# Both products of a block join over four 32x32 tiles instead of two, a state update with 48 stationary columns, and an order of work planned anew

## The chip, the cores and the metric

The kernel runs on one core of a Trainium2 chip. The metric is the device time of one execution in microseconds (us), here the median of three runs. The engines named below are TensorE (PE; its weight loads, which overlap the matmuls, are listed as PEld), VectorE (DVE), ScalarE (ACT), GpSimd (POOL) and SyncE (SP). SP computes nothing and issues most of the DMA transfers.

## The reference

Four batches, eight heads, 768 tokens, head size 48, all in float32. A DeltaNet layer keeps one 48x48 state per batch and head and goes through the tokens in order:

```
k_n = k / (norm(k) + 1e-6)
for t in range(S):
    y[t]  = q[t] @ state
    v_old = state.T @ k_n[t]
    state = state + beta[t] * outer(k_n[t], v[t] - v_old)
```

The heads of `y` are then laid side by side (4 x 768 x 384), and a MetaFormer block with an identity mixer follows: normalise each token over its 384 numbers, multiply by `g_ln`, `relu(xn @ w_ch1) @ w_ch2` with a hidden width of 1536, and add `y` back.

## The kernel before

**Chunks.** The tokens are cut into 12 chunks of 64. Inside a chunk the recurrence becomes matrix products for each of the 32 batch-and-head pairs ("heads" from here on): with the state S at the chunk's start, `ks = K S` and `qs = Q S` (line 1160), `u = X (v - ks)` (line 1215), `y = qs + P u` (line 1222), and `S += K^T u` (line 1232, the function `state_up`). P is the masked product of queries and keys (`queries`, line 963), and X is the inverse of a unit triangular 64x64 matrix built from the chunk's keys and beta (`gram`, line 963). Heads lie in two halves of 64 partitions, 16 heads (`GH`) to a half. On tiles of 64x64 of the TensorE array, two halves by two, each of these products is 32 matmuls in the source; the trace has two records for every float32 matmul, so a product appears as 64, and below it is said to have 64.

**The inverse.** For chunks 2 to 11 two chunks are inverted together in `rows_inverse`. The 64x64 triangle is cut into two 32x32 diagonal blocks and one block beside them. The diagonal blocks of two chunks are laid one to a partition by DMA (64 heads times two blocks), and VectorE inverts them row by row with a multiply (line 1045, into `tmp`) and a subtract (line 1050, into `xb`), 31 pairs for a block of 32. The planner counts each pair as one step. The result goes back to the layout of the products through DRAM (`xd<-xb`, then eight transfers `xt<-xd`).

**The join.** `join(c)` then fills the remaining 32x32 block: a transpose on VectorE (line 1103), a product E (line 1110), an eviction with a change of sign on ScalarE into `es` (line 1120), a product Z (line 1115) and an eviction into `xt` (line 1125). Each product is again 64 recorded matmuls: 16 heads by two halves, the halves named by `e`, and two records for each. `quad(n)` is the n-th group of 32 partitions. All inputs of E lie in quads 0 and 2. All its outputs go to quads 1 and 3 of one PSUM bank:

```
for h in range(GH):
    for e in range(2):
        nc.tensor.matmul(p[quad(2 * e + 1), h], gs[quad(2 * e), h, BK:C], xnj[quad(2 * e), h])
```

So E uses two of the array's 32x32 tiles, and Z, from quads 1 and 3 to quads 0 and 2, two others. Each product is evicted in two instructions of 32 partitions by 512 elements. Chunks 1 to 11 go through `join`. Chunk 1 also has `blocks_join`, which works one level lower, on 16x16 inverses; its two products of 128 recorded matmuls (lines 1077 and 1082) already run over four 32x32 tiles, from quad a to quad a. Chunk 1's own product `u` goes partly (line 1184) from quads 1 and 3, each to both of quads 1 and 3, with 48 moving columns.

**The MLP.** Chunks 0 to 2 use a plain first layer (line 1483). From chunk 3 on the first layer runs in `eleven` (line 1416) and from chunk 1 on the second in `seven` (line 1584), schemes that replace matmuls by sums on VectorE, ScalarE and GpSimd. They consist of full 128x128 matmuls on TensorE.

**The order of the work.** Every instruction is given to a planner (`Line`) as a step with an engine, an assumed cost, the buffers that it reads and writes, and optionally a due time. `schedule` goes backward from the due times (`DUE`, one for each chunk's MLP, and a slope) to a priority `pr` for each step; `run` then simulates the engines, the DMA queues, a port that it takes VectorE and GpSimd to share, and the fetching of TensorE's instructions (`BLOCK`, `FETCH`, `STALL`), and at each moment picks the ready step with the earliest `pr`. The order found is the order of the instructions in each engine's queue. On the chip each engine then works strictly in that order. Line 1662 is a dummy product on zeros that the planner puts where TensorE would sit idle early in the kernel. Line 555 is the helper that issues all DMAs.

## Time and profile before

| | |
|---|---|
| time, median of three runs | 560.05 us (558.03 to 564.31) |
| span of the profiled execution | 559.0 us |
| TensorE busy | 525.5 us, 94% of the span |
| VectorE, GpSimd, ScalarE busy | 370.3, 253.2 and 192.1 us |
| mean granted TensorE clock | 0.980 |
| DMA traffic | 54.65 MB, 98 GB/s |

The page of the profile gives busy time for each engine, the span in 40 slices of 14 us each, the chain of work that ended last, and groups of instructions by line. A row of such a group names the line, the engine, what is written and from what, the shape, the count, the busy time, the mean duration in nanoseconds of one instruction and the idle time before it. Small matmuls are pipelined: one takes 0.19 us from start to end, but the next starts a few nanoseconds later, so what a product of 64 of them costs is read from its first start and last end, not from the mean duration of one.

### The profile page before, as it was taken

The numbers are of one execution on the slowest core, as the hardware profiler recorded it, in microseconds if no ns is written. First come the engines' busy times: TensorE is split into PE (matmuls) and PEld (weight loads), VectorE is DVE, ScalarE is ACT, GpSimd is POOL, SyncE is SP. The second block draws the span as 40 slices with busy tenths as digits, with TensorE's granted clock in tenths as the row PEclk, the third lists the DMA queues.
The fourth block names the chain that finished last, engine by engine and source line by source line (L and its number), as shares of the span: only waits on it lengthen the run. The fifth ranks groups of instructions, "written<-read, shape, count | busy, mean of one in ns | idle before, by whom it ended". The sixth has DMA issues, their size and how long they took to land.

```text
span 559.0 us, 23060 instructions
## 1 busy us (share of the span) xinstructions
PE 525.5 (94%) x10060; PEld 478.8 (86%) x10060; DVE 370.3 (66%) x884; ACT 192.1 (34%) x452; POOL 253.2 (45%) x399
## 2 busy tenths in 40 slices
PE   7668869899998999899999999999999999999996
PEld 4547657678987899899999999999999999999996
DVE  5666549991689936889858968668777436253331
ACT  5667644232232324232323332513322224323030
POOL 5252337407885656267270352452352522426242
PEclk9898899999998999899999999999999999999999
DMA  9784784269454786553652543834404410111101
GB/s 177 265 158 128 195 219 64 44 149 168 55 86 71 139 195 86 106 100 83 162 77 50 99 81 77 191 46 81 94 15 103 106 30 33 32 48 40 28 1 28
DMA packets 195972, 54.65 MB, mean 98 GB/s; under 512 B 186136, under 2 KB 189344, under 8 KB 195872
## 3 DMA queue, kind: packets, MB, share of 16 engines
q1 hardware_dynamic: 190112, 40.39, 37.8%
q10 hardware_dynamic: 3552, 9.63, 5.0%
q0 software_dynamic: 2208, 3.17, 3.2%
q8 instruction: 78, 1.28, 1.0%
q14 instruction: 22, 0.18, 0.1%
HBM read 36.38 MB, written 16.78 MB: 95 GB/s over the span
## 4 chain that ended last, share of the span: by engine, by line
PE 78%; DVE 7%; DMA 6%; SPq 4%; issue 2%; ACT 1%; POOL 0%; DVEq 0%; POOLq 0%; ACTq 0%
PE f L1584 28%; PE f L1416 25%; PE f L1483 6%; SPq L555 4%; PE two L963 4%; DVE xb L1050 2%; DVE tmp L1045 2%; PE by L1222 2%; PE two L1215 2%; PE by L1160 2%; PE two L1160 2%; DMA gd<-gsb 2%; PE two L1232 2%; PE f L1505 1%; PE by L1115 1%
## 5 line engine op out<-in xcount | busy, mean ns | idle before, releaser
L1584 PE MATMUL f<-w_sb,h_all 128*128 128x192 f32 x396 | 95.0, 332 | 0.0
L1584 PE MATMUL f<-words,h_all 128*128 128x192 f32 x396 | 93.1, 328 | 0.0
L1570 POOL TENSOR_TENSOR h_all<-h_all 128x256 f32<-128x256 f32 x99 | 73.0, 742 | 43.3 <-PE f L1584 37.1
L1416 PE MATMUL f<-xnt,w_sb 128*128 128x128 f32 x648 | 88.8, 279 | 0.0
L1609 POOL TENSOR_TENSOR words<-h_all 128x128 f32<-128x128 f32 x66 | 30.3, 472 | 121.0 <-ACT h_all L1435 101.5
L1416 PEld LDWEIGHTS f<-xnt,w_sb 128*128 128x128 f32 x648 | 81.0, 193 | 0.7
L1438 DVE TENSOR_TENSOR h_all<-f,h_all 128x256 f32<-128x256 f32 x135 | 56.5, 421 | 34.1 <-PE f L1416 20.2
L1050 DVE TENSOR_TENSOR xb<-xb,tmp 128x60 f32<-128x60 f32 (+19 forms) x170 | 73.4, 432 | 5.8
L1045 DVE TENSOR_TENSOR tmp<-xb,gb 128x60 f32<-128x60 f32 (+19 forms) x170 | 65.3, 384 | 7.1 <-POOL xb L1034 4.5
L1584 PEld LDWEIGHTS f<-words,h_all 128*128 128x128 f32 x396 | 68.3, 190 | 0.4
L1584 PEld LDWEIGHTS f<-w_sb,h_all 128*128 128x128 f32 x396 | 66.4, 190 | 1.6 <-issue 0.2
L1483 PE MATMUL f<-xnt,w_sb 128*128 128x256 f32 x216 | 51.7, 390 | 0.0
L1483 PEld LDWEIGHTS f<-xnt,w_sb 128*128 128x128 f32 x216 | 41.3, 195 | 7.2
L555 POOL DMA_DIRECT2D tb<-in_k_dram x64 | 41.7, 656 | 7.0 <-DVE kt L943 5.8
L1602 DVE TENSOR_TENSOR o<-f,x 128x192 f32<-128x192 f32 x33 | 11.7, 355 | 47.7 <-PE f L1584 28.4
L1435 ACT ACTIVATE h_all<-f 128x256 f32<-128x256 f32 x54 | 20.6, 381 | 53.8 <-PE f L1416 28.0
L1584 PE MATMUL f<-w_sb,words 128*128 128x192 f32 x132 | 32.5, 330 | 0.6 <-DVE o L1602 0.6
L1602 POOL TENSOR_TENSOR o<-o,words 128x192 f32<-128x192 f32 x22 | 13.3, 624 | 38.6 <-DVE words L1602 38.6
L1492 ACT ACTIVATE h_all<-f 128x256 f32<-128x256 f32 x36 | 13.8, 383 | 38.2 <-PE f L1483 38.0
L1435 ACT ACTIVATE h_all<-h_all 128x256 f32<-128x256 f32 x54 | 22.2, 413 | 11.3 <-DVE h_all L1438 11.2
L748 POOL TENSOR_TENSOR w_sb<-words 128x768 uint32<-128x768 uint32 (+1 forms) x11 | 14.9, 1356 | 24.3 <-ACT words L738 19.4
L825 POOL TENSOR_TENSOR v<-v,knrm 128x768 f32<-128x768 f32 x11 | 16.7, 1518 | 16.7 <-DMA v<-in_v_dram 16.0
(235 smaller groups left out, 941.3 us busy)
## 6 DMA issues: line engine op xcount, KB each, us to landing
words<-in_moe_w_ch_dram ACTq DMA_DIRECT2D x10, 768.0 KB, 7.2
gd<-gsb SPq DMA_DIRECT2D x11, 512.0 KB, 3.9
v<-in_v_dram SPq DMA_DIRECT2D x24, 192.0 KB, 4.2
out_dram<-o SPq DMA_DIRECT2D x48, 96.0 KB, 2.3
kr<-in_k_dram SPq DMA_DIRECT2D x46, 96.0 KB, 3.0
xld<-xlt SPq DMA_DIRECT2D x9, 384.0 KB, 3.7
xnt<-xld SPq DMA_DIRECT2D x36, 96.0 KB, 3.0
gb<-gd SPq DMA_DIRECT2D x40, 64.0 KB, 3.7
```

The source lines that it names most:

```text
L555: add(eng, cost, lambda: QUEUE[eng].dma_start(out=out_, in_=in_), r, w, bulk=n * ns / 16e3, **kw)
L963: nc.tensor.matmul(pair[hp][half(e ^ (hp & n)), (g * NP + j) * C : (g * NP + j + 1) * C], kt[drows(hp), l], rt[drows(hp), i],)
L1045: nc.vector.tensor_tensor(out=t, in0=xv[:, 0:n, j : j + 1].to_broadcast([128, n, w]), in1=gv[:, j : j + 1, j + 1 : L].to_broadcast([128, n ...
L1050: nc.vector.tensor_tensor(out=rest, in0=rest, in1=t, op=ALU.subtract)
L1416: nc.tensor.matmul(wide(p[:, 128 * n : 128 * n + 128]), w[:, f : f + 128], r, start=start and n == 0, stop=stop, skip_group_check=True)
L1435: add("ACT", act(256), lambda: nc.scalar.activation(to[0], p, ACTF.Relu), pk, to[1])
L1438: add("DVE", dve(256), lambda: nc.vector.tensor_tensor(out=to[0], in0=ps(p), in1=y[0], op=op), [*pk, *y[1]], to[1])
L1483: nc.tensor.matmul(p[:, 0:TOK], w1_sb[:, t, f * 128 : (f + 1) * 128], xnt[:, t], start=(t == 0), stop=(t == KC - 1))
L1570: add(eng, cost, lambda: e.tensor_tensor(out=out_, in0=x, in1=y, op=op), r, w, port=2 if eng == "Pool" else 1, pr=-2)
L1584: lambda f=f, t=start and f == 0: nc.tensor.matmul(p[:, 0:D2], lhs(f), rhs[:, f], start=t, stop=(f == F2 - 1), skip_group_check=True),
L1602: lambda: e.tensor_tensor(out=out_, in0=a, in1=b_, op=ALU.add), r, w, pr=pr,
L1609: lambda f=f + i: e.tensor_tensor(out=s3[f], in0=one(0, 0)[0](f), in1=one(1, 0)[0](f), op=ALU.subtract),
```

## The change

There are three parts.

**The join's products over four tiles.** In each product half of the heads (`g` = 0) keeps its output quad, and the other half (`g` = 1) writes to the quad beside it, so E's two input quads feed four output quads, and likewise Z's. The number of matmuls stays the same. The eviction puts the halves back where they belong: four instructions of 32 partitions by 256 elements in place of two by 512. Both products now claim the whole bank instead of one half of it each.

**The state update.** From chunk 1 on `state_up` loads 48 stationary columns for each head instead of 64; the 16 columns left out were padding, and the sum into `s_all` still runs over all 128 partitions. Chunk 0 keeps 64.

**The planner.** The multiply and the subtract of `rows_inverse` become two steps, so that others can be placed between them. A four-tile product is costed at `QUARTER` a matmul, the state update at 0.85 us. A step can have a cap on its priority (`cap`): the `xt<-xd` transfers of each pair of chunks and the `u` product of each chunk from 2 on have one. Ties between steps go to the one whose engine is free first, a wait on the shared port is costed 0.1 us shorter, and the planner's constants and due times are other numbers. So the order on every queue is another.

```diff
-PASS = 0.0165
+PASS, QUARTER = 0.0165, 0.0092
...
-    HOP, GIVE, PATIENCE, SLACK, EAGER = 0.17, 0.1, 0.8, 3.0, 0.0
+    HOP, GIVE, PATIENCE, SLACK, EAGER = 0.17, 0.075, 0.694, 3.372, 0.068
...
-    URGENT, STALL = 6.0, 0.25
-    PE_TAIL, SWITCH = 0.12, 0.1
+    URGENT, STALL = 6.0, 0.278
+    PE_TAIL, SWITCH, OVERLAP = 0.12, 0.1, 0.1
...
-                    if t is not None and (best is None or t < best[0]):
-                        best = (t, e)
+                    if t is not None and (best is None or (t, max(free[e], rd)) < best[:2]):
+                        best = (t, max(free[e], rd), e)
...
+            cost = s.cost
             if e in ports:
-                ports[e] = (t + s.cost, s.port)
+                until, kind = ports["Pool" if e == "DVE" else "DVE"]
+                if s.port and kind + s.port > 2 and t < until + 1e-9:
+                    cost -= self.OVERLAP
+                ports[e] = (t + cost, s.port)
...
-            s.pr = min(late + [s.due if s.due is not None else 1e6])
+            s.pr = min(late + [x for x in (s.due, s.cap, 1e6) if x is not None])
...
+    def four(n, fn, r, w, **kw):
+        return add("PE", n * QUARTER, fn, r, w, np=n, arr=0.0017 * n, **kw)
...
-            add("DVE", 2 * dve(n * w), row, gbk, ["xb"], port=1, **kw)
+            add(
+                "DVE", dve(n * w),
+                lambda j=j, n=n, w=w, t=t: nc.vector.tensor_tensor(
...
+                [*gbk, "xb"], ["tmp"], port=1, **kw,
+            )
+            add(
+                "DVE", dve(n * w), lambda t=t, rest=rest: nc.vector.tensor_tensor(out=rest, in0=rest, in1=t, op=ALU.subtract),
+                ["tmp"], ["xb"], port=1, **kw,
+            )
...
-        pe(128, prod_e, gk + XN, ATT, 0.22, **kw)
+        four(128, prod_e, gk + XN, ATT, **kw)
...
+        spread_ = [(e, g) for g in range(2) for e in range(2)]
+        heads = [slice(H * g, H * g + H) for g in range(2)]
+
         def prod_e():
-            for h in range(GH):
-                for e in range(2):
-                    nc.tensor.matmul(p[quad(2 * e + 1), h], gs[quad(2 * e), h, BK:C], xnj[quad(2 * e), h])
+            for j in range(H):
+                for e, g in spread_:
+                    h = H * g + j
+                    nc.tensor.matmul(p[quad(2 * e + 1 - g), h], gs[quad(2 * e), h, BK:C], xnj[quad(2 * e), h])
...
+                    nc.tensor.matmul(p[quad(2 * e + g), h], es[quad(2 * e + 1), h], xt[quad(2 * e + 1), h, c0 : c0 + BK])
...
-        pe(64, prod_e, gk + [("xn", 0), ("xn", 1)], [ATT[1]], 0.11, name=f"e{c}", **kw)
-        for e in range(2):
-            rows = quad(2 * e + 1)
-            add("ACT", act(512), lambda rows=rows: nc.scalar.mul(es[rows], p[rows], -1.0), [ATT[1]], [("es", e)], **kw)
+        four(64, prod_e, gk + [("xn", 0), ("xn", 1)], ATT, name=f"e{c}", **kw)
+        for e, g in spread_:
+            add(
+                "ACT", act(256),
+                lambda e=e, g=g: nc.scalar.mul(es[quad(2 * e + 1), heads[g]], p[quad(2 * e + 1 - g), heads[g]], -1.0),
+                ATT, [("es", e, g)], **kw,
+            )
+        four(64, prod_z, [("es", e, g) for e, g in spread_] + xq, ATT, name=f"z{c}", **kw)
+        for e, g in spread_:
+            add(
+                "ACT", act(256), lambda e=e, g=g: nc.scalar.copy(xt[quad(2 * e), heads[g], BK:C], p[quad(2 * e + g), heads[g]]),
+                ATT, [("xo", c % NX, e, g)], **kw,
             )
...
-            pe(64, prod_u, ["qs", *vk, *xt_keys(c)], TWO, 0.65, name=f"u{c}", **kp_e)
+            pe(64, prod_u, ["qs", *vk, *xt_keys(c)], TWO, 0.65, name=f"u{c}", cap=cap(c + 3), **kp_e)
...
-            p_s = p_2
+            p_s, w = p_2, D if c else DP
...
-                        p_s[half(hp), e, j], kp[half(e ^ hp), h0 * DP : h0 * DP + DP], us[half(e ^ hp), h0]
+                        p_s[DP * hp : DP * hp + w, e, j], kp[half(e ^ hp), h0 * DP : h0 * DP + w], us[half(e ^ hp), h0]
...
-            pe(64, state_up, raw_keys(c) + [("u", 0), ("u", 1)], TWO, 0.65, name=f"s{c}", **kp_e)
+            add("PE", 0.85 if c else 1.06, state_up, raw_keys(c) + [("u", 0), ("u", 1)], TWO, np=64, arr=0.65, name=f"s{c}", **kp_e)
...
-    DUE = [44.40, 70.70, 90.32, 129.22, 162.45, 201.63, 231.70, 268.25, 308.70, 351.43, 392.84, 417.04, 2.36, 1.27, 1.35, 26.71]
+    DUE = [48.277, 71.786, 106.38, 130.403, 162.437, 198.122, 232.536, 276.844, 291.162, 352.992, 380.582, 403.451, 2.36, 1.205, 1.373, 25.345]
+    CAP = [80.445, 119.235, 215.61, 300.648, 367.636, 84.616, 102.629, 176.88, 201.93, 209.915, 265.167, 304.028, 344.354, 363.114, 424.868]
...
-            add("PE", 0.43, go, [*wk, *rk], pk, due=due(c, t0[0]), np=4, arr=0.43)
-            t0[0] += 0.43
+            add("PE", 0.448, go, [*wk, *rk], pk, due=due(c, t0[0]), np=4, arr=0.448)
+            t0[0] += 0.448
```

More of the change, by code (lines that the diff above doesn't have):

```diff
@@ L65 @@
 ENGS = ("PE", "Pool", "DVE", "ACT", "SP")
[L66 removed]
+PASS, QUARTER = 0.0165, 0.0092
 class Step:
     __slots__ = (
[L71 removed]
+        "eng", "cost", "fn", "deps", "pr", "lag", "bulk", "start", "end", "n", "users", "name", "t0", "np", "arr", "hold", "ready", "least", "due", "port", "banks", "cap"
     )
 class Line:
[L79 removed]
+    HOP, GIVE, PATIENCE, SLACK, EAGER = 0.17, 0.075, 0.694, 3.372, 0.068
     PSUM = ("two", "by", "f0", "f1", "f2", "f3")
[L81 to L82 removed]
+    URGENT, STALL = 6.0, 0.278
+    PE_TAIL, SWITCH, OVERLAP = 0.12, 0.1, 0.1
     BLOCK, FIRST, FETCH = 128, 93, 3.95
@@ L91, in __init__, with add @@
         self.readers = {}
-    def add(self, eng, cost, fn, r=(), w=(), pr=0.0, lag=0.0, bulk=None, name="", t0=0.7, after=(), np=0, arr=0.0, hold=None, due=None, port=0):
+    def add(self, eng, cost, fn, r=(), w=(), pr=0.0, lag=0.0, bulk=None, name="", t0=0.7, after=(), np=0, arr=0.0, hold=None, due=None, port=0, cap=None):
         s = Step()
@@ L293, in run @@
                 continue
-            t, e = best
+            t, _, e = best
             now = []
@@ L344, in run @@
             else:
-                free[e] = s.end = t + s.cost
+                free[e] = s.end = t + cost
             for b in s.banks:
@@ L1348, in due, with cap @@
         return DUE[c] + DUE[12 + min(c, 2)] * t
+    def cap(i):
+        return CAP[i]
     def w1_part(i, k):
```

37 lines of the change are left out of this document (14 added, 23 removed).

## The prediction

> **What bounds the kernel.** I read first the busy shares, the slices and the shares of the chain on the page, then stretches of the span.
>
> ```profile
> PE 525.5 (94%) x10060; PEld 478.8 (86%) x10060; DVE 370.3 (66%) x884; ACT 192.1 (34%) x452; POOL 253.2 (45%) x399
> ...
> PE   7668869899998999899999999999999999999996
> ...
> PE 78%; DVE 7%; DMA 6%; SPq 4%; issue 2%; ACT 1%; POOL 0%; DVEq 0%; POOLq 0%; ACTq 0%
> ```
>
> TensorE is busy 94% and holds 78% of the chain that ended last. The first seven slices (98 us) are weaker than the rest, so I cut the span there and where the profile changes again:
>
> ```profile
> core 0: us, PE busy (x) PEld busy (x) DVE busy (x) ACT busy (x) POOL busy (x), PEclk, DMA share, GB/s
> 0.00:90.00 90.00, 68.24 (x1699) 53.81 (x1700) 56.47 (x158) 56.34 (x119) 36.62 (x53) 0.92 0.75 180
> 90.00:175.00 85.00, 80.50 (x1592) 65.13 (x1591) 64.71 (x138) 23.49 (x57) 50.70 (x75) 0.98 0.56 99
> 175.00:490.00 315.00, 312.14 (x6297) 295.94 (x6296) 224.85 (x527) 98.20 (x237) 139.24 (x226) 0.99 0.45 89
> 490.00:554.60 64.60, 64.59 (x478) 63.93 (x476) 23.89 (x62) 14.04 (x39) 26.64 (x46) 1.00 0.10 25
> ```
>
> From 175 to 490 us TensorE idles 2.9 us in 315, and from 490 to 554.6 not at all. There any TensorE time that goes brings the end forward by the same amount, as long as the recurrence still feeds the MLP. Before 175 it is otherwise. The chain in order of time (start, duration, what) shows both:
>
> ```profile
> 148.12 1.13 PE f L1110 x64
> ...
> 152.04 1.13 PE f L1115 x64
> ...
> 157.37 1.13 PE f L1110 x64
> ...
> 165.34 1.14 PE two L963 x64
> 166.50 1.23 DVE pt L994
> ...
> 170.70 0.40 DVE xln L1278
> ...
> 171.24 1.38 PE by L1310 x6
> 172.62 2.56 PE f L1662 x6
> 175.18 1.39 PE f L1483 x6
> ...
> 215.18 1.03 PE f L1115 x58
> 216.31 0.92 PE f L1110 x59
> ...
> 486.65 1.08 PE by L1222 x64
> 487.73 4.10 PE f L1584 x24
> ...
> 540.71 13.89 PE f L1584 x84
> ```
>
> At 172.6 TensorE runs the dummy product of line 1662: it has no MLP work until chunk 2's normalised output has been turned (line 1310), which waited for VectorE's `xln`. So up to 175 us the recurrence sets the pace. Afterward it runs ahead: its last product ends at 487.73, and 66.9 us of MLP follow. That distance is the cushion for anything that delays a late chunk.
>
> **Part 1, the join's products.** The nearest operations are already in the trace. The timeline gives start, duration and count of a block, and the answers on line 1110 the least, median and greatest ns of one matmul:
>
> ```profile
> 88.12 1.29 PE L1082 MATMUL by<-xt,es 32*32 32x32 f32 x128
> ...
> 102.61 0.54 PE L1184 MATMUL two<-v,xt 32*32 32x48 f32 x32
> ...
> 373.16 1.20 PE L1110 MATMUL by<-xnj,gsb 32*32 32x32 f32 x64
> ```
>
> ```profile
> L1110 PE MATMUL by<-xnj,gsb x384: 191/191/212, 292.3 to 471.7; 32*32 32x32 f32 x192
> L1110 PE MATMUL f<-xnj,gsb x320: 191/191/212, 93.9 to 217.0; 32*32 32x32 f32 x160
> ```
>
> One matmul takes 0.19 us from start to end. A two-tile product therefore starts one every (1.20 - 0.19)/63 = 16.0 ns. The four-tile product of line 1082 has the same shape and starts one every (1.29 - 0.19)/127 = 8.7 ns. In it every input quad feeds one output quad, however, while in the change two input quads feed two each. Line 1184 does just that, with 48 moving columns instead of 32: (0.54 - 0.20)/31 = 11.0 ns, 0.20 us for one being my estimate, a little over the 0.191 of 32 columns. So a product falls from 1.20 us to between 0.19 + 63 x 8.7 ns = 0.74 us and 0.19 + 63 x 11.0 ns = 0.88 us. I take the first, since its shape is the same: 0.46 us saved, at worst 0.32, at best 0.50 (half of 63 x 16.0 ns).
>
> The 384 + 320 matmuls are 11 products E; with the 11 products Z that is 22. Of the 11 chunks, 1, 2 and 3 are joined before 175 us (line 1110 at 93.9, 148.1 and 157.4), which leaves 16 products in the stretch that TensorE bounds: 16 x 0.46 = **7.4 us** (5.1 to 8.0). Of the six earlier products, the four of chunks 2 and 3 lie on the chain, 1.8 us, but VectorE ends the wait behind them. I take half, **0.9 us** (0 to 1.8), and nothing for chunk 1.
>
> **Part 2, the state update.** Rows of the chain, the timeline and the groups for stationary against moving columns:
>
> ```profile
> 383.73 1.08 PE two L1215 x64
> ...
> 388.32 0.93 PE two L1232 x64
> ```
>
> ```profile
> 388.14 1.11 PE L1232 MATMUL two<-u,kr 64*64 64x48 f32 x64
> ```
>
> ```profile
> L1232 PE MATMUL two<-u,kr 64*64 64x48 f32 x704 | 13.8, 227 | 1.9 <-issue 1.9
> ```
>
> Line 963 streams 64 columns against 64 stationary ones in 1.14 us or less (above), line 1215 streams 48 against 64 in 1.08: with 64 stationary columns the moving ones hardly count. Line 1184, 48 against 32, goes at 11.0 ns; line 1232, at 0.227 us for one, now at (1.11 - 0.23)/63 = 14.0. If the larger of the two numbers counts, 48 against 48 goes at 11.0 ns and saves 63 x 3.0 ns = 0.19 us; if the tile is loaded in full all the same, nothing. I take 0.19, as the rows agree with the larger number. Ten updates change (chunks 1 to 10), eight of them after 175 us (chunks 3 to 10): **1.5 us** (0 to 1.6).
>
> **Part 3, ScalarE's evictions.** The groups of ScalarE by shape:
>
> ```profile
> L1432 ACT COPY h_all<-f 128x256 f32<-128x256 f32 x27 | 10.0, 371 | 24.3 <-PE f L1416 24.1
> L1120 ACT ACTIVATE es<-by 32x512 f32<-32x512 f32 x12 | 7.1, 589 | 21.8 <-PE by L1110 21.7
> L1125 ACT COPY xt<-by 32x512 f32<-32x512 f32 x12 | 6.9, 575 | 13.8 <-PE by L1115 13.7
> ```
>
> Two of 0.58 us become four of 0.37: +0.32 us per product, 22 x 0.32 = 7.0 us on an engine that is busy 98 of 315 us there. The step from E through the eviction to Z gets 0.46 - 0.32 = 0.14 us shorter. Queued behind the extra 0.32 us are ScalarE's copies out of the MLP's banks (lines 1432, 1435), and TensorE waits for those banks; it has four, so I put it at **0**. Without that cover it would be 16 x 0.32 = 5.1 us. Both products now claim the whole bank, so a second chunk's E must also wait for the first chunk's `xt` copies, up to 4 x 0.37 = 1.5 us. Only one E (216.31, above) comes right behind another chunk's Z. There the planner needs MLP work in between, which it has; cost 0.
>
> **Part 4, the order.** Splitting multiply and subtract adds no instruction on VectorE. What the new order does to TensorE's idle time the trace doesn't show. It moves every queue, SP's and GpSimd's too. After 175 us it can fill 2.9 us at most; before, there is the hole at 166 to 175, shown by the busy time of line 1662 alone:
>
> ```profile
> 90.00:176.00 86.00, 5.04 (x14) 3.26 (x14) 0.98 0.56 98
> ```
>
> So 5.0 us of dummy products, beside 4.5 us of idle time from 90 to 175. In the first 90 us TensorE idles for 21.8 us. As the cap pulls chunk 2's `u` and the scatter before it forward, I expect a part of the hole to be filled, **1.5 us** (from a gain of 9.5, all of both, to a loss as large, since no row excludes a worse order).
>
> **Part 5, instruction fetch.** Two stalls after 142 us wait for nothing that the profile shows:
>
> ```profile
> 161.49 0.90 PE L1232 MATMUL two<-u,kr 64*64 64x48 f32 x44 [0.39 <-issue]
> ```
>
> ```profile
> 225.21 1.01 PE L1232 MATMUL two<-u,kr 64*64 64x48 f32 x51 [1.55 <-issue]
> ```
>
> ```profile
> q8 instruction: 78, 1.28, 1.0%
> ```
>
> Both sit inside a product, where small products stand close together, and 10060 recorded matmuls in 78 packets are 129 to a packet. A packet is used up faster when products shrink. I put a loss of **0.5 us** on it (a gain of 1.9 if both stalls go, a loss of 4 if two or three more like the longer one come). The Trainium skill, page "Runtime: NRT & Kernel Launch", section "Instruction fetch mechanics", holds that fetching is mostly hidden because instructions are issued more slowly than they are fetched. By that this term would be 0 and the sum 0.5 us lower; the 1.55 us stall speaks against it.
>
> **The sum.** 7.4 + 0.9 + 1.5 + 1.5 - 0.5 = 10.8 us. The profiled span is 559.0 us, so 548.2; the median of the runs shown, 560.05, lies 1.05 above the span, so **549.2 us**.
>
> **The rivals.**
>
> *The order fills the front (a).* The same savings, and the new order removes all 5.0 us of dummies after 90 us and a fifth of the 21.8 us idle before: 5.0 + 4.4 in place of 1.5, so 549.2 - 7.9 = **541.3 us**. For it: TensorE is idle or on dummies for 31 us before 175. Against: what it waits for there is a chain of transfers and VectorE steps of which only the order changes.
>
> *The tiles don't run side by side (b).* Two input quads would feed four output quads one after the other, so a product stays at 1.20 us, and ScalarE's 0.32 us are left. Without the 8.3 us of part 1 it is **557.5 us**. Line 1184 speaks against it, at 11.0 ns with two inputs feeding two outputs each. The Trainium skill, page "TensorEngine Tiling (Array Packing)", "Gotcha 1: PSUM Pressure", states that different row tiles cannot access the same PSUM bank at once; that would give this time. Line 1082 writes one bank from four row tiles at 8.7 ns, so the trace doesn't agree.
>
> *The gain goes into stalls (c).* Denser small products run out of fetched instructions, or the MLP's banks wait for ScalarE. Three stalls of 1.55 us, or the uncovered 5.1 us of part 3: 549.2 + 5 = **554 us**. For it: the stall at 223.7; against: the mean distance of packets, 559/78 = 7.2 us.
>
> *Slower: a scatter queued behind a store (d).* SP works in order, and its list is new:
>
> ```profile
> SPq L555 <- POOL o L1602: 106.8, 9, 24.7
> ```
>
> Nine times SP stood before an output store that needed GpSimd's sum, once for 24.7 us. Late in the kernel the 66.9 us cushion hides it. Before 175 us nothing does: if the loads or `xt<-xd` scatters of chunks 2 to 4 stand behind such a store, TensorE runs dummies for as long. With 24.7 us it is 549.2 + 24.7 = **574 us**. From 10.8 us on the change gains nothing, from 16.5 us on it is slower by 1%.
>
> **How the numbers follow.** About 1% (5.6 us) is what a measurement of this kernel tells from no change: 554.4 and 565.7 are the bounds. The forecast (545 to 552) gets 0.54, (a) 0.12, (c) 0.14, (b) 0.07, (d) 0.13. The range leaves out the far side of (a) and (d): 541 to 558. Faster by over 1%: the forecast, (a) and the better two thirds of (c), 0.75. Within 1%: the rest of (c), (b), and a short wait of (d), 0.15. Slower: 0.10.
>
> **What would show it.** Lines 1110 and 1115 in blocks of 64 that take 0.74 us from first start to last end; 0.92 us for line 1232; ScalarE's rows 32x256 at 0.37 us, 88 of them; TensorE's busy time lower by about 11 us, VectorE's the same; "issue" on TensorE under 3 us after 142 us; fewer dummies after 166 us, and the first product of chunk 2's MLP (line 1483, now 175.2) about 2 us earlier. The prediction is wrong if blocks stay at 1.2 us (b), if the busy time falls but idle time after 175 grows beyond 5 us (c), or if that first product comes after 180 us (d).

## The result and the profile after

The changed kernel takes **550.96 us** (median of four runs, 549.73 to 554.20), the kernel before 560.41 us beside it (four runs, 558.03 to 564.31). The ratio is **0.9873 [0.9833, 0.9914]**, a gain of 4.8 to 9.4 us. Two further comparisons of the same two kernels gave 0.9896 [0.9844, 0.9949] and 0.9883 [0.9841, 0.9924], so the gain is nearer to 6 or 7 us than to the 9.4 us between the first two medians. 549.2 us had been predicted, and a span of 548.2 us.

The page of the changed kernel: the span, busy times, TensorE's slices and the shares of the chain that ended last.

```profile
span 548.0 us, 23151 instructions
...
PE 517.9 (95%) x10068; PEld 468.9 (86%) x10068; DVE 368.0 (67%) x884; ACT 200.0 (36%) x496; POOL 255.3 (47%) x399
...
PE   7769979999959999999999999999999999999996
...
PE 67%; DVE 13%; DMA 4%; SPq 4%; issue 3%; ACT 1%; DVEq 0%; ACTq 0%
```

TensorE's busy time fell by 525.5 - 517.9 = 7.6 us, where about 11 had been predicted, and the span by 11.0; VectorE's hardly moved (370.3 to 368.0), and ScalarE's rose by 7.9. The slices are at 9 from the thirteenth (164 us) to the last but one, but the twelfth (151 to 164 us) is now a 5: the hole ahead of chunk 2's MLP has moved and not gone. VectorE's share of the chain rose from 7% to 13%; from 141 to 176 us, in the hole, its time on the chain grew from 4.6 to 19.8 us, and the rest of the rise stands elsewhere.

The lines have moved: E 1110 is now 1125, Z 1115 is 1131, the state update 1232 is 1250, ScalarE's `es` and `xt` copies 1120 and 1125 are 1137 and 1143, the dummy product 1662 is 1684, and the MLP's first products 1416 and 1483 are 1438 and 1505. The timeline of the changed kernel (start, duration, what) gives the blocks:

```profile
364.75 0.75 PE L1125 MATMUL by<-xnj,gsb 32*32 32x32 f32 x64
368.68 0.75 PE L1131 MATMUL by<-xt,es 32*32 32x32 f32 x64
379.12 0.90 PE L1250 MATMUL two<-u,kr 64*48 64x48 f32 x64
```

E and Z take 0.75 us for 1.20, the state update 0.90 for 1.11. ScalarE's evictions by shape, with mean ns of one and the idle time before them:

```profile
L1137 ACT ACTIVATE es<-by 32x256 f32<-32x256 f32 x24 | 9.0, 374 | 13.9 <-PE by L1125 13.7
L1143 ACT COPY xt<-by 32x256 f32<-32x256 f32 x24 | 8.7, 362 | 8.8 <-PE by L1131 8.5
L1137 ACT ACTIVATE es<-f 32x256 f32<-32x256 f32 x20 | 7.5, 374 | 25.2 <-PE f L1125 24.9
L1143 ACT COPY xt<-f 32x256 f32<-32x256 f32 x20 | 7.3, 363 | 4.8 <-PE f L1131 4.6
```

That is 88 evictions at 0.37 us, as foreseen. Next I cut the span where chunk 2's MLP begins, which is at 172.2 us now and was at 175.0 before. From there to TensorE's last end, with the columns of the prediction's table, first the changed kernel and then the kernel before from its own 175.0 on:

```profile
172.20:543.70 371.50, 368.90 (x6772) 350.38 (x6772) 244.23 (x588) 118.79 (x310) 166.97 (x272) 1.00 0.40 80
```

```profile
175.00:554.60 379.60, 376.73 (x6773) 359.87 (x6771) 248.75 (x589) 112.25 (x276) 165.88 (x272) 1.00 0.39 78
```

Of the 11.0 us, 379.6 - 371.5 = 8.1 come after that cut, 2.8 before it and 0.1 after TensorE's last end. In this stretch TensorE idles 2.6 us (2.9 before) and is busy 368.9 us (376.7 before): 7.8 of the 8.1 us are busy time that went. The same stretch for one line at a time (columns: length, TensorE's busy time with its matmuls, weight loads, granted clock, DMA share, GB/s), first E before (Z has the same row), then the state update before:

```profile
175.00:554.60 379.60, 9.60 (x512) 8.71 (x512) 1.00 0.39 78
175.00:554.60 379.60, 9.23 (x512) 8.45 (x512) 1.00 0.39 78
```

and E, Z and the state update of the changed kernel:

```profile
172.20:543.70 371.50, 6.33 (x512) 5.36 (x512) 1.00 0.40 80
172.20:543.70 371.50, 6.03 (x512) 5.14 (x512) 1.00 0.40 80
172.20:543.70 371.50, 7.24 (x512) 6.53 (x512) 1.00 0.40 80
```

3.27 + 3.57 + 1.99 = 8.8 us less busy time in the three products, where 7.4 + 1.5 = 8.9 were predicted. TensorE as a whole is busy 7.8 us less there; where the other 1.0 us went was not taken apart.

The place before the cut went otherwise than predicted. The busy time of the dummy product between 90 and 176 us is more than twice what it was (5.04 us before):

```profile
90.00:176.00 86.00, 11.17 (x40) 7.65 (x40) 0.96 0.56 97
```

The chain of the changed kernel in order of time shows what TensorE waits for:

```profile
157.57 2.54 DVE xb L1061
...
162.52 0.96 DVE s_all L1260
...
165.51 3.17 PE f L1684 x10
...
172.22 1.56 PE f L1505 x6
```

VectorE's row steps (line 1061) stand ahead of `s_all` in its list, and two of them take over 2 us (2.11 and 2.53). TensorE waits 4.8 us for `s_all`, and the wait is followed by a lower clock: from 150 to 172.2 us it was granted at 0.85 (0.94 from 150 to 175 us before), and the product behind the wait, line 970, takes 1.98 us where it (then line 963) took 1.16 before:

```profile
163.53 1.98 PE L970 MATMUL two<-qt,kt 48*64 48x64 f32 x64 [4.82 <-DVE s_all L1260]
```

So the new order did not fill this hole but widened it. What it did fill is the front. The first 90 us of the changed kernel, its dummies there, and the dummies there before:

```profile
0.00:90.00 90.00, 73.03 (x1839) 56.61 (x1843) 60.08 (x177) 58.04 (x124) 40.12 (x60) 0.92 0.80 183
0.00:90.00 90.00, 5.58 (x20) 3.39 (x20) 0.92 0.80 183
```

```profile
0.00:90.00 90.00, 11.99 (x38) 6.89 (x38) 0.92 0.75 180
```

TensorE's work without dummies is 73.03 - 5.58 = 67.5 us in the first 90 us, against 68.24 - 11.99 = 56.3 before; from 90 to 176 us it is 68.6 against 76.5. The order moved about 11 us of work to the front and gave about 8 of them back in the hole. Two further profiles of the changed kernel and one of the kernel before (below) show the same: 64.9 and 67.1 us in the first 90, against 55.1. What lengthens the row steps, and whether the 2.8 us by which chunk 2's MLP begins earlier are the order's, is for the experiments.

### The profile page after: what moved, and what is told of

Same layout as the page of the kernel before. It is cut to its first block, busy times and chain, and to the rows that moved or that the text cites. A ratio compares the mean times of both kernels' runs of the same rounds, so it can differ in the third digit from the quotient of the medians.

```text
span 548.0 us, 23151 instructions
## 1 busy us (share of the span) xinstructions
PE 517.9 (95%) x10068; PEld 468.9 (86%) x10068; DVE 368.0 (67%) x884; ACT 200.0 (36%) x496; POOL 255.3 (47%) x399
## 4 chain that ended last, share of the span: by engine, by line
PE 67%; DVE 13%; DMA 4%; SPq 4%; issue 3%; ACT 1%; DVEq 0%; ACTq 0%
PE f L1606 25%; PE f L1438 24%; DVE xb L1061 4%; SPq L559 4%; DVE tmp L1054 3%; PE f L1505 3%; PE two L970 3%; PE two L1178 2%; PE by L1178 2%; DMA xt<-xd 2%; PE by L1240 1%; PE two L1233 1%; DMA words<-in_moe_w_ch_dram 1%; PE f L1684 1%; PE two L1250 1%
## 5 line engine op out<-in xcount | busy, mean ns | idle before, releaser
L1606 PE MATMUL f<-words,h_all 128*128 128x192 f32 x396 | 90.1, 329 | 0.1
L1054 DVE TENSOR_TENSOR tmp<-xb,gb 128x60 f32<-128x60 f32 (+19 forms) x170 | 69.1, 407 | 3.2
L1457 ACT ACTIVATE h_all<-h_all 128x256 f32<-128x256 f32 x54 | 21.9, 413 | 17.3 <-DVE h_all L1460 17.2
L1606 PEld LDWEIGHTS f<-w_sb,words 128*128 128x128 f32 x132 | 22.6, 190 | 1.4 <-DVE o L1624 1.1
```

Source lines behind the costliest of these rows:

```text
L1054: lambda j=j, n=n, w=w, t=t: nc.vector.tensor_tensor(out=t, in0=xv[:, 0:n, j : j + 1].to_broadcast([128, n, w]), in1=gv[:, j : j + 1, j + ...
L1457: add("ACT", act(256), lambda: nc.scalar.activation(to[0], p, ACTF.Relu), pk, to[1])
L1606: lambda f=f, t=start and f == 0: nc.tensor.matmul(p[:, 0:D2], lhs(f), rhs[:, f], start=t, stop=(f == F2 - 1), skip_group_check=True),
```

## The experiments

My theory: the shorter products bring 6 to 9 us where TensorE sets the pace, ScalarE's extra work and the new order bring and cost nothing that the time shows. Its rivals: the order carries a good part of the gain, the gain is lost where products run out of fetched instructions, ScalarE's extra work is about to cost something, and the order is a risk that this one version happens to have avoided. "P" below is the start of chunk 2's MLP, "R" the time from there to TensorE's last end; before they are 175.0 and 379.6 us, after 172.2 and 371.5.

**One part at a time.** *e1_join_only*: the four-tile products and the four evictions in the kernel before, with its planner's order; one E is put behind the other chunk's `xt` copies, which now use the same bank.

```
-            for h in range(GH):
-                for e in range(2):
-                    nc.tensor.matmul(p[quad(2 * e + 1), h], gs[quad(2 * e), h, BK:C], xnj[quad(2 * e), h])
+            for j in range(H):
+                for e, g in spread_:
+                    h = H * g + j
+                    nc.tensor.matmul(p[quad(2 * e + 1 - g), h], gs[quad(2 * e), h, BK:C], xnj[quad(2 * e), h])
...
+        def both_es(e):
+            for g in range(2):
+                nc.scalar.mul(es[quad(2 * e + 1), heads[g]], p[quad(2 * e + 1 - g), heads[g]], -1.0)
```

> The order of the kernel before on every queue, with the join's products over four tiles and their evictions in four instructions; state update and planner as before (one product moves behind the copies whose bank it now shares). Theory, that TensorE's time is the bound after chunk 2's MLP has begun and what the tiles save there is saved at the end: blocks of lines E and Z at 0.68 us instead of 1.13, 16 of them after that point, so 7 us, and up to 2 us before it: 551.5 to 553.5 against 560.4, with the first matmul of chunk 2's MLP at 174 to 175.2 us. Rival, that the new order gives the gain: 559 to 561.

Measured: 552.58 us against 557.40, ratio 0.9917 [0.9883, 0.9952]. The gain is smaller than expected. The stretch from P on, and two rows of the timeline with the idle time ahead of them in brackets:

```profile
173.20:547.70 374.50, 370.23 (x6773) 352.80 (x6772) 249.78 (x590) 117.55 (x310) 165.99 (x272) 1.00 0.39 79
```

```profile
161.17 0.90 PE L1242 MATMUL two<-u,kr 64*64 64x48 f32 x44 [0.78 <-issue]
...
224.31 1.46 PE L1242 MATMUL two<-u,kr 64*64 64x48 f32 x51 [1.56 <-issue]
```

Busy time falls by 376.7 - 370.2 = 6.5 us, but the idle time in that stretch rises from 2.9 to 4.3: beside the long stall at 223, which the kernel before has too, short waits stand there. One, of 0.7 us, is an E that waits for another chunk's `xt` copies out of the bank that they now share, for which part 3 had put 0; e3 and e7 have it too. Another, of 0.9 us, is a wait for one of the MLP's banks; the second profile of the kernel before (e9) has it as well, so it is not the edit's. The stall at 161 (0.39 before) has doubled and lies ahead of the stretch. With the old order a part of the gain goes into waits, in kind as rival (c) has it: 1.4 us more idle time than in the first profile of the kernel before, 0.9 more than in e9 (3.4).

*e2_state_only*: the 48 stationary columns alone, in the kernel before.

```
-            p_s = p_2
+            p_s, w = p_2, D if c else DP
...
-                        p_s[half(hp), e, j], kp[half(e ^ hp), h0 * DP : h0 * DP + DP], us[half(e ^ hp), h0]
+                        p_s[DP * hp : DP * hp + w, e, j], kp[half(e ^ hp), h0 * DP : h0 * DP + w], us[half(e ^ hp), h0]
```

> The kernel before with 48 stationary columns in the state update of chunks 1 to 10, nothing else. Theory: 0.21 us for each of 8 updates after chunk 2's MLP has begun and at most 0.4 us before: 558.3 to 558.8 against 560.4. Rival, that the shorter block only moves the wait for the sum into the state: no change, 560.4.

Measured: 556.14 against 557.40, ratio 0.9978 [0.9949, 1.0008]: 1.3 us where 1.6 to 2.1 had been expected, and the time alone does not tell it from no change. The timeline does tell the block, 0.90 us for 1.11, and R falls by 2.1 us to 377.5 (by 0.9 against e9's 378.4, below):

```profile
386.33 0.90 PE L1232 MATMUL two<-u,kr 64*48 64x48 f32 x64
```

*e3_both_old_order*: the edits of e1 and e2 together, the old order kept.

```
...
-            p_s = p_2
+            p_s, w = p_2, D if c else DP
...
```

> Both of the two above in the order of the kernel before. Theory: the two gains add up, 9 to 11 us, so 549.5 to 551.5, as fast as the changed kernel. Rival, that the order planned anew has a share of its own: slower than the changed kernel by 2 us or more, 553 to 556.

Measured: 551.53 against 557.40, ratio 0.9896 [0.9855, 0.9936]. The gain of the changed kernel is there without its order, though at 5.9 us it is smaller than the 9 to 11 expected. R is 371.8 us, and P stays at 175.5:

```profile
175.50:547.30 371.80, 367.79 (x6773) 349.60 (x6772) 247.27 (x589) 116.86 (x308) 166.34 (x272) 1.00 0.39 80
```

P doesn't show whether the four joins of chunks 2 and 3, for which 0.9 us had been written down, bring anything: it varies by more than that between profiles of one kernel (below). A stretch inside one profile does. From chunk 2's E to the product of line 963 the chain of the kernel before takes 165.34 - 148.12 = 17.2 us (rows in the prediction), and e9 17.2 too. In e3:

```profile
149.62 0.75 PE L1116 MATMUL f<-xnj,gsb 32*32 32x32 f32 x64
...
165.84 1.16 PE L963 MATMUL two<-qt,kt 48*64 48x64 f32 x64 [0.50 <-DVE qt L943]
```

That is 16.2 us, as in e1, which has the joins alone, although the stall in it is longer. So the joins do bring 1.0 us there; the rest goes into the stall and a wait for VectorE (0.50). Whether the 1.0 us reach the end was not resolved.

*e4_order_only*: the changed kernel with the two-tile products, the two wide evictions (each booked at the first of the two places, the second left empty) and 64 stationary columns.

```
-            for j in range(H):
-                for e, g in spread_:
...
+            for h in range(GH):
+                for e in range(2):
+                    nc.tensor.matmul(p[quad(2 * e + 1), h], gs[quad(2 * e), h, BK:C], xnj[quad(2 * e), h])
...
-            p_s, w = p_2, D if c else DP
+            p_s, w = p_2, DP
```

> The order of the changed kernel with the products over two tiles, evictions in two instructions and 64 stationary columns. Theory: only the 3.0 us by which chunk 2's MLP begins earlier, less what the slower products before it cost: 557 to 560. Rival, that the order carries the gain: 549 to 552. Second rival, that an order planned for short products suits long ones badly: above 561.

Measured: 557.25 against 557.40, ratio 1.0001 [0.9970, 1.0033]. The order alone gains nothing that the time shows, where up to 3 us had been expected, though P is at 171.6 us; R is 378.8:

```profile
171.60:550.40 378.80, 376.99 (x6772) 358.99 (x6772) 246.45 (x588) 113.35 (x278) 168.05 (x272) 1.00 0.38 78
```

e3 and e4 together settle where the gain is from: 1.04% without the order, 0.0% by the order alone, and 1.0 to 1.3% with both.

**The two references again.** *e5_changed_again* and *e12_changed_third* are the changed kernel and *e9_before_again* is the kernel before, without an edit.

> The changed kernel as it is, beside the kernel before on the same chip. Theory: 8 us from chunk 2's MLP on, 0 to 3 us before it, so a ratio of 0.981 to 0.989. Rival, that the order's 3.0 us before that point are real in every execution: 0.980 to 0.982.

> The changed kernel once more, beside the one above on the same chip: 0.984 to 0.990 of the kernel before, chunk 2's MLP from 172 to 174 us.

> The kernel before, profiled a second time, as a measure of how far two profiles of one kernel differ. Theory: from the first matmul of chunk 2's MLP to TensorE's end 379.6 us within 1 us, as in the first profile; the start of that matmul (175.0 us in the first profile) may move by 1 to 2 us with the transfers ahead of it. Rival: the second part varies as much as the first, and differences of 1 us in it mean nothing.

Measured: 551.32 against 557.46 and 551.06 against 557.40, the ratios given above; the profiled execution of e9 took 561.91 us. P is 173.3, 174.6 and 177.4 us, R is 371.2, 370.9 and 378.4. So P varies by 2.4 us between profiles of one kernel, R by 0.6 to 1.2. The 2.8 us that the first pair of profiles shows ahead of P are hardly more than that, the 8 us behind P are far more. Both profiles of the kernel before also fell on slower executions: time less span is 1.7 us in the profiled executions of e9 and of the changed kernel, so the first, with a span of 559.0, took about 560.7 us, and e9 took 561.91, where the median of the kernel before is 556.6 to 557.5 beside the experiments. (Some of this lies just outside what was expected: 0.9896 above 0.989, P at 174.6 behind 174, and differences of 2.4 and 1.2 us in P and R where at most 2 and 1 were.)

**ScalarE's cover.** *e6_scalar_doubled*: the changed kernel with each of its 88 evictions cut into two of 128 columns.

```
+        def parts(g):
+            return [slice(H * g + NP * n, H * g + NP * n + NP) for n in range(2)]
...
-                lambda e=e, g=g: nc.scalar.mul(es[quad(2 * e + 1), heads[g]], p[quad(2 * e + 1 - g), heads[g]], -1.0),
+                lambda e=e, g=g: [nc.scalar.mul(es[quad(2 * e + 1), x], p[quad(2 * e + 1 - g), x], -1.0) for x in parts(g)],
```

> The changed kernel with each of the join's 88 evictions cut into two of 32x128, the order of all else as it was: by the rows 32x256 at 0.374 us and 32x512 at 0.589 us, one of 128 columns takes about 0.27 us, so ScalarE works 88 x 0.16 = 14 us more, 0.64 us more between each E and its Z. Theory, that MLP work on TensorE covers it: within 1 us of the changed kernel, 0.980 to 0.990 of the kernel before. Rival, that TensorE waits for ScalarE's banks: 5 to 10 us slower than the changed kernel.

Measured: 549.50 against 557.46, ratio 0.9848 [0.9798, 0.9897], where the changed kernel had 0.9896 [0.9844, 0.9949] on the same chip: no cost. The evictions of one E in this kernel and in the changed one, and its stretch from P on:

```profile
366.53 1.75 ACT L1140 ACTIVATE es<-by 32x128 f32<-32x128 f32 x8 [6.49 <-PE by L1128]
```

```profile
365.55 1.53 ACT L1137 ACTIVATE es<-by 32x256 f32<-32x256 f32 x4 [5.97 <-PE by L1125]
```

```profile
173.50:544.50 371.00, 368.56 (x6773) 350.46 (x6772) 244.21 (x588) 122.52 (x374) 167.99 (x272) 1.00 0.39 80
```

One of 128 columns takes 0.26 us from start to end, but eight in a row take 1.75 us and not 2.1: they overlap. So the edit adds 0.22 us to a product and not the 0.64 expected, and ScalarE is busy 3.7 us longer from P on, not some 10. TensorE idles 2.4 us there as it did (2.3 to 2.6). The copies out of the MLP's banks have that much room; more was not put to the test.

**Instruction fetch.** *e7_fetch_shifted*: e3 with one dummy product at the start of the kernel replaced by 33 small ones, which puts 64 more recorded matmuls ahead of all that follows.

```
+            if early:
+                for i in range(33):
+                    nc.tensor.matmul(ps[quad(i % 4), 0:8], nought[quad(i % 4), 0:32], nought[quad(i % 4), 0:8])
+                return
```

> The third kernel above (both parts, old order) with one dummy product at the start replaced by 66 tiny records, so that every later record stands 64 places further along. Theory, that the stalls which wait for nothing visible come where one packet of 128 records ends before the next has landed: the stalls of 0.86 and 1.06 us inside the state updates of chunks 2 and 4 leave these products, and any that remain sit 64 records away. Rival, that they belong to these products: they stay where they are. Time within 2 us of the third kernel.

Measured: one execution, 553.62 us, P 172.6, R 374.9. The stalls of e3 in the timeline, and those of e7 (its lines 1236, 1126 and 1430 are the products y and Z and one of the MLP's):

```profile
162.10 0.74 PE L1242 MATMUL two<-u,kr 64*48 64x48 f32 x44 [0.85 <-issue]
...
224.43 0.83 PE L1242 MATMUL two<-u,kr 64*48 64x48 f32 x51 [1.06 <-issue]
```

```profile
160.05 0.84 PE L1236 MATMUL by<-u,pt 64*64 64x48 f32 x42 [1.23 <-issue]
163.36 0.59 PE L1126 MATMUL f<-xt,es 32*32 32x32 f32 x45 [1.39 <-issue]
222.07 0.96 PE L1236 MATMUL by<-u,pt 64*64 64x48 f32 x50 [1.01 <-issue]
226.97 0.60 PE L1430 MATMUL f<-pt,w_sb 128*128 128x128 f32 x4 [1.62 <-issue]
```

Both stalls left the state update and went to y, the product 64 records ahead of it. Counted from the start of the trace they stay behind the same record, the 3022nd and the 4425th, in the kernel before, in e3 and in e7; e7 has new ones behind the 3149th (in Z), the 4552nd (in the MLP) and the 4680th (0.78 us, in line 1174), 127 or 128 records after the one before. A wait for data or for a bank would have stayed with its product. A stall that stays with the count of records is one of the fetched packets.

The traces say more when all of TensorE's instructions are counted, weight loads and the rest included, and the landings of the packets of queue q8 (16,384 bytes each) are set beside them. After 142 us the fourteen traces of this document have 36 waits that the profile puts to "issue", of 0.17 to 2.11 us. All 36 stand at the same place of a run of 256 instructions (a multiple of 256 plus 193 or 194), and all end 1.2 to 1.7 us after a packet has landed. So these waits are the fetch. They stand in small products or right behind them: in none of the traces do two packets land less than 3.29 us apart after 142 us, and 64 recorded matmuls of a four-tile product, half a packet with their weight loads, are done in 0.75 us.

**The order as a risk.** *e10_no_caps*: the changed kernel with the caps of the planner left out.

```
-        return CAP[i]
+        return None
```

> The changed kernel without the caps on priorities, so with its due times and constants alone; another order, the same instructions. The planner puts its end 8.5 us later than that of the changed kernel. Theory, that the order decides only where chunk 2's MLP begins and how often TensorE idles after it: that matmul starts later than 173 us or idle time after it is above 2.5 us, and the sum of the two accounts for the time, 553 to 558 where the kernel before has 557.5. Rival, that the caps do nothing on the chip: within 1 us of the changed kernel.

Measured: 560.75 us against 556.62, ratio **1.0071 [1.0040, 1.0102]**: slower, by 4 us, with all the shorter products in it, and later than the 553 to 558 expected. Its stretch from P on, one stall of its timeline, and its dummy products from 90 to 176 us:

```profile
175.60:554.60 379.00, 371.48 (x6780) 352.31 (x6772) 244.09 (x584) 117.70 (x308) 168.84 (x272) 1.00 0.39 78
```

```profile
166.89 0.25 PE L1131 MATMUL f<-xt,es 32*32 32x32 f32 x3 [2.11 <-issue]
```

```profile
90.00:176.00 86.00, 15.90 (x44) 10.10 (x44) 0.92 0.55 97
```

Against the mean of the changed kernel's three profiles R is 379.0 - 371.2 = 7.8 us longer and P 2.2 us later, so most of the loss lies behind P. TensorE idles 7.5 us there instead of 2.6, and 4.4 of them (0.5 in the changed kernel) are waits for fetched packets as above; a stall of 2.1 us is back ahead of P. That is the place of rival (c). TensorE is also busy 2.6 us longer from P on; that was not taken apart.

Ahead of P the dummies have grown to 15.9 us at a granted clock of 0.92. There the scatters `xt<-xd` are late on SP: they run from 137.3 to 143.6 us, and from 130.8 to 135.0 in the changed kernel. VectorE's last row step and SP's write `xd<-xb` behind it, in the changed kernel and then in e10, show why:

```profile
122.46 0.21 DVE L1061 TENSOR_TENSOR xb<-xb,tmp 128x31 f32<-128x31 f32 x1
...
124.32 0.43 SPq L559 DMA_DIRECT2D xd<-xb  x1
```

```profile
131.34 0.21 DVE L1061 TENSOR_TENSOR xb<-xb,tmp 128x31 f32<-128x31 f32 x1
...
131.74 0.43 SPq L559 DMA_DIRECT2D xd<-xb  x1
```

The inversion itself ends 8.9 us later. That fits the edit: the caps on the scatters are gone, and with them what gave the row steps ahead of them an early priority. Loads that SP takes among the scatters add about 1 us. So this is not rival (d), a scatter that stands behind an output store.

*e8_new_numbers*: the changed kernel with due times, caps and constants found anew, by which the planner's own end comes 4.8 us earlier.

```
-    HOP, GIVE, PATIENCE, SLACK, EAGER = 0.17, 0.075, 0.694, 3.372, 0.068
+    HOP, GIVE, PATIENCE, SLACK, EAGER = 0.17, 0.077, 0.878, 2.697, 0.072
...
-    CAP = [80.445, 119.235, 215.61, 300.648, 367.636, 84.616, 102.629, 176.88, 201.93, 209.915, 265.167, 304.028, 344.354, 363.114, 424.868]
+    CAP = [83.503, 119.444, 216.187, 301.083, 376.696, 84.458, 101.302, 176.028, 201.93, 209.915, 265.004, 301.945, 344.354, 364.616, 418.172]
```

> The changed kernel with other due times, caps and five other constants of the planner, so another order again, all instructions the same. The planner puts its end 4.8 us earlier than that of the changed kernel. Theory, that the order is worth only what it takes out of the hole before chunk 2's MLP and of TensorE's idle time after it (2.5 us): 0 to 4 us faster than the changed kernel, 0.975 to 0.987 of the kernel before. Rival, that an order found on the planner's numbers doesn't hold on the chip: slower than the changed kernel.

Measured: 549.91 against 557.46, ratio 0.9866 [0.9818, 0.9914], not to be told from the changed kernel's 0.9896 on the same chip. P is 174.7 and R 371.7. The planner's 4.8 us are not in the trace: the wait for `s_all` is 5.2 us, as in two of the changed kernel's three profiles (4.8, 5.2, 5.2), and a stall of 1.06 us is back at 225.7.

**What widens the hole.** The timeline of the changed kernel where TensorE waits for `s_all`, VectorE and GpSimd side by side:

```profile
157.57 2.53 DVE L1061 TENSOR_TENSOR xb<-xb,tmp 128x220 f32<-128x220 f32 x1
...
157.90 1.01 POOL L1394 TENSOR_TENSOR qt<-w_sb 128x384 f32<-128x384 f32 x1
...
158.85 1.00 POOL L1394 TENSOR_TENSOR pt<-w_sb 128x384 f32<-128x384 f32 x1
...
160.14 0.40 DVE L1054 TENSOR_TENSOR tmp<-xb,gb 128x231 f32<-128x231 f32 x1
```

A row step beside GpSimd's sums of the weights (line 1394) takes 2.53 us, the next one, between two sums, 0.40. *e11_sums_later*: those sums may start from 175 us instead of 150, and due times, caps and constants are found anew for that.

```
-                    [ak[n], bk[n]], [ok[n]], after=() if last else gone, t0=150.0,
+                    [ak[n], bk[n]], [ok[n]], after=() if last else gone, t0=175.0,
```

> The changed kernel with GpSimd's sums of the first layer's weights (two columns of work that only chunk 3's MLP needs) allowed from 175 us on instead of 150, and due times and caps found anew for that; all instructions the same. Theory, that VectorE's row steps of 1.1 to 2.5 us at 151 to 162 us, behind which the sum into the state waits, are long because GpSimd's sums run beside them: without these the same steps take 0.4 us, TensorE's 4.8 us wait for the sum shrinks below 2 us and chunk 2's MLP begins at 169 to 171 us instead of 172.2 to 173.5; time 0.975 to 0.985 of the kernel before. Rival, that the row steps are long for another reason: they stay above 1 us and the time within 1 us of the changed kernel.

Measured: 549.98 against 557.40, ratio 0.9849 [0.9800, 0.9899], beside 0.9883 [0.9841, 0.9924] of the changed kernel on the same chip: not told apart. In its timeline and its waits:

```profile
156.87 0.39 DVE L1061 TENSOR_TENSOR xb<-xb,tmp 128x220 f32<-128x220 f32 x1
```

```profile
PE f L1438 <- ACT xnt L1322: 2.2, 1, 2.2
PE f L1606 <- DVE o L1624: 2.1, 2, 1.9
...
PE two L970 <- DVE s_all L1260: 1.6, 2, 1.4
```

```profile
167.40:543.30 375.90, 367.88 (x6781) 350.12 (x6772) 253.60 (x587) 117.48 (x308) 172.62 (x278) 1.00 0.39 79
```

The same row step takes 0.39 us. The six pairs of row steps from 128x175 to 128x240 take 12.1 us in the changed kernel (150.49 to 162.61) and 6.0 in e11 (152.99 to 159.02), where one step is still long: 1.50 us beside GpSimd's product of line 832. That GpSimd's work lengthens the row steps is shown; most of it is the sums. The wait for `s_all` falls from 4.8 to 1.4 us, and P comes at 167.4, earlier than the 169 to 171 expected and than all three profiles of the changed kernel (172.2 to 174.6). That the hole shrinks because of the row steps rests on e11 alone, whose order differs in more than the sums: `s_all` stands behind two more pairs there and begins 1.3 us earlier (161.2 for 162.5), and the rest of the gain comes behind it. The 4.8 us by which P comes earlier than in the first profile are given back behind it: TensorE idles 375.9 - 367.9 = 8.0 us there, the longest times for a normalised input (2.2), an output sum (1.9) and a fetched packet (1.3). Here an MLP that starts earlier waits more later.

## Why the prediction was right, and where not

**Parts 1 and 2 were right in mechanism and size.** E and Z went from 1.20 to 0.75 us (0.74 predicted), the state update from 1.11 to 0.90 (0.92 predicted). From P on 8.8 us of these products' busy time went where 8.9 had been written (6.8 for 7.4 in the joins, 2.0 for 1.5 in the update), 7.8 of TensorE's as a whole, and R fell by 8.1 us, since nothing else came to bound it. The rule that the larger of the stationary and the moving columns counts is borne out by the 0.90 us of 48 against 48. Rival (b), tiles that do not run side by side, falls with the 0.75 us: line 1125 has two row tiles that write one bank, with starts (0.75 - 0.19)/63 = 8.9 ns apart, and so the rule of the Trainium skill, page "TensorEngine Tiling (Array Packing)", "Gotcha 1: PSUM Pressure", does not agree with this trace either, as line 1082 had already said.

**The 0.9 us for the joins of chunks 2 and 3** came about in the old order, where the products stand on the chain: 17.2 us became 16.2 in e1 and e3. It doesn't show in the totals, since the front varies by more: chunk 2's E begins at 148.0 us in one profile of the kernel before and at 151.9 in the other.

**Part 3 was right for this order.** 88 evictions at 0.37 us and 7.9 us more of ScalarE's time cost nothing that shows, and e6 shows that 3.7 us more would not either. The shared bank, also put at 0, costs 0.7 to 0.8 us in the old order (e1, e3, e7) and nothing in the new one.

**Part 4 failed in its mechanism.** "A part of the hole to be filled" was the step; the dummies there went from 5.0 to 11.2 us instead, with GpSimd's weight sums beside VectorE's row steps. What the order filled is the first 90 us, by about 11 us of work, and the hole gave most of that back. The prediction could have seen more room there than it did: its 31 us of idle time and dummies before 175 us leave out the 12.0 us of dummies in the first 90. P still came earlier in the profiles (172.2, 173.3 and 174.6 against 175.0 and 177.4), which is about 2.8 us on the mean, but both profiles of the kernel before are of slower executions, and the timed runs give the order nothing: 1.0001 [0.9970, 1.0033] alone, and e3 has 0.9896 without it. Whether it is worth a part of the 1.5 us lies below what was resolved, and stays open.

**Part 5 had its sign wrong for this order, and its mechanism right.** Neither of the two stalls (1.94 us together) is in the changed kernel after 142 us, where a loss of 0.5 was predicted; two short ones of 0.25 us are. That is luck of this order: e8 and e10, with the same products, have stalls of over 1 us again (1.06 in e8, 1.30 and 2.11 in e10). With the old order they stayed at 0.85 and 1.06 us (e3) or 0.78 and 1.56 us (e1). The Trainium skill, page "Runtime: NRT & Kernel Launch", section "Instruction fetch mechanics", holds that fetching is mostly hidden; e7, where the stalls keep to the instruction count at 0.8 to 1.6 us each, does not agree with that here. (By that rule the savings would have summed to 0.5 us more, not less as the prediction has it.)

**The sum.** 10.8 us had been predicted. The two profiles differ by 11.0, and the median is within 1.8 us of the forecast, but this flatters it: over the three comparisons the kernel is 5.8 to 7.1 us faster (1.04% of 557 to 1.27% of 560), and their intervals end at 8.7, 8.9 and 9.4, all below 10.8. That the time itself came so near is partly luck: the kernel before had 560.4 us in the first comparison and 556.6 to 557.5 in the later ones. R alone gives 379.0 - 371.2 = 7.8 us on the mean of the profiles, so nothing measurable is left for the 0.9 + 1.5 = 2.4 us ahead of P. The 8.9 - 0.5 = 8.4 us of the other terms lie inside the intervals of all three.

**The rivals.** (a) came by half: of the 21.8 us idle in the first 90, 4.8 went, the fifth that it had named, and 6.4 of the 12.0 us of dummies there. But the 5.0 us of dummies after 90 grew by 6.1, so nothing of it shows at the end. (b) fell with part 1. (c) is real where the order is not matched to the products: e10 lost 4.4 us to fetched packets behind P. (d) was not seen in the changed kernel or in e10; that an order can make the same products slower than before is shown (e10, by 0.7%), but by other waits than a scatter behind a store.

## What to carry to other kernels

Take a saving at its full size only in the stretch where the engine that it relieves has no idle time: here 8.1 us came through for 8.8 us that the products got shorter, and of 2.4 us forecast ahead of that stretch nothing showed in the time. A product of small tiles is worth spreading until every output quad has its own work, and the evictions that this multiplies cost nothing while their engine has room. Test a planner's new order without the other edits, and the edits without the order, since a planned gain of 4.8 us can be absent from the chip (e8) and a missing constraint can cost more than the edit brings (e10). Compare stretches inside one profile before whole profiles: the front of the kernel before moves by up to 4 us from one profile to the next, R by about 1.

## What the runs showed of the hardware

- A VectorE operation with two inputs in SBUF is held up by GpSimd's: 0.39 us alone (e11), 2.53 us beside two sums of 1.0 us, ending 0.25 us behind the second of them (158.85 + 1.00 against 157.57 + 2.53). The Trainium skill, page "SBUF — State Buffer", section "SBUF: two separate sides", describes a pair of ports that the two engines share by a lock for a whole instruction, which goes to the one that starts first. The trace agrees that VectorE waits for whole operations of GpSimd; it doesn't show the second part, since VectorE's step is recorded 0.33 us before the first of the sums (157.57 against 157.90) and waits for both.
- TensorE's waits for "issue" after 142 us stand at fixed counts of its instructions, 256 apart or a multiple of that, and end 1.2 to 1.7 us after an instruction packet of 16,384 bytes has landed (36 of 36 waits, 0.17 to 2.11 us, in fourteen traces). An edit at the start of the kernel moves them from one product to another (e7).
- The state update, 64 recorded matmuls in float32, takes 1.11 us with 64 stationary and 48 moving columns, and 0.90 us with 48 and 48.
- After 4.8 us in which TensorE had nothing, 64 matmuls that take 1.16 us took 1.98, and the clock granted from 150 to 172.2 us was 0.85. After 3.3 us in e4 they took 1.99.
